# A linear-attention block and a feed-forward block in one kernel: the hand-written order of steps extended to the fifth turn

## The chip, the cores and the metric

The kernel runs on one core of a Trainium2 chip. A core has five engines with a queue each, taken strictly in order: TensorE (PE in the profile, its weight loads PEld), VectorE (DVE), ScalarE (ACT), GpSimd (POOL) and SyncE (SP), which here issues most of the transfers. The metric is the device time of one execution in microseconds (us), the median of several runs. The profile is one execution taken by the hardware profiler.

## What is computed

Per head a decaying state is updated token by token and read by a query; the result, with the heads side by side, is the input of a feed-forward block with an unusual activation.

```python
# q, k, v, f_logit: (4, 8, 768, 48), float32
f = 1.0 / (1.0 + np.exp(-f_logit))
for t in range(S):
    state = f[:, :, t, :, None] * state + np.einsum('bhd,bhe->bhde', k[:, :, t], v[:, :, t])
    y[:, :, t] = np.einsum('bhd,bhde->bhe', q[:, :, t], state)
# x: y as (3072, 384); w_in (384, 2048) and w_out (2048, 384), float64
h = x @ w_in
sp = np.maximum(h, 0.0) + np.log1p(np.exp(-np.abs(h)))
g = h * erf(sp)
out = (g @ w_out).astype(np.float32)
```

All products are made in float32.

## The kernel before

**Tiles.** The 4 x 768 tokens are 24 *chunks* of 128 tokens, numbered g; a batch has six of them. Two chunks make a *block* of 256 tokens, of which there are 12; a block's 2048 hidden columns are four *groups* of 512, and a group is made in two halves.

**Attention of a chunk.** The logits are clamped (`clamp`, DVE), turned into logarithms of the decay (ACT), and summed along the chunk by a product with a triangle (`log_sums`, PE). `decays` (ACT) makes factors from the sums, which `times_q` and `times_k` (DVE) put on the rows of q and k. Both are transposed (PE) and copied out of PSUM (`copy_q` on ACT, `copy_k`). `state_products` and `scores` (PE) make what goes into the state and the products of keys and queries; the scores are masked into `qA` (`masks`: either a masked product on DVE, or copies on ACT with a select on POOL). `add_state` (DVE) carries the state across half chunks, with the decay totals in `Tall`; `copy_state` (POOL) puts it beside v in `sv`. `x_rows` (PE, tile y) makes the rows, `copy_x` (ACT) puts them into `xT`. The totals come either from a small product (`sum_totals`) or from eight small transfers (`send_totals`, SP).

There are whole and *tiled* forms of the sums and transposes. The whole ones use the array of 128 x 128 at once, with many zeros in it (`log_sums`: one matmul of 384 columns; `transposes`: four of 128 x 128 each for q and k). The tiled ones use 64 x 64 quarters or 64-row halves (`tiled_sums`: four matmuls of 192 columns; `tiled_transposes`: sixteen of 64 columns). Tiled transposes write into a pair of PSUM banks of which there is one (`bank_pair`); `open_pair` exchanges the two single banks for it. Tiled sums need logits in another layout, which `load_f` makes with four transfers instead of one, and they use one of the two places (`ps_moe`) in which the hidden products and the output are summed.

**Feed-forward of a block.** `half_group` makes half a group of hidden columns (6 matmuls of 256 columns, tile hps); `copy_h` copies the group out (ACT); the activation takes one exp, two tanh terms and a last tanh on ACT, two combining products and a last product on DVE (`act_steps`, in turns by `act_step`). The output of blocks 0 and 1 is made directly (`project_first`, L865: 32 matmuls of 384 columns). From block 2 on `project` (L916) needs seven products of 192 columns where eight would be due; for that DVE makes sums of weights (`sum_w`) and of hidden values (`sum_h`).

**Weights** come as 16 pieces of float64 words and are rounded to float32 in seven steps each, one on ACT and six on DVE (`round_piece`).

**What sets the order.** Up to the third block an order of steps is written out by hand (`EARLY`, 454 names such as `d4` for the sums of chunk 4 or `h0_1` for a half group of block 0); it fixes each engine's queue. Behind it the loop `for it in range(2, n_blocks)` runs *turns*: turn it makes the output of block it-2 and the hidden columns of block it+1, matmul by matmul; at fixed slots of a turn it sets attention stages (`stage_d` to `stage_y`, later `burst`), loads, activation steps, sums and rounding steps. Turns 2 and 3 have rules of their own: they still round weights, use `project_first`, and pass from whole to tiled forms.

## Time and profile before

| | us |
|---|---|
| timed runs | 604.35, 605.14, 607.07; median 605.14 |
| the profiled execution: its time | 603.14 |
| the profiled execution: its span | 601.4 |
| last end of an ACT instruction of the activation | about 557 |

The span goes from the first to the last instruction of the program; what lies between it and the execution's time is start and end of the execution. In the profile, a line such as `L765` is a line of the kernel; `out<-in` are tiles. A matmul of float32 shows as two records, a transpose as one. Busy time of PE counts a matmul's full length, although matmuls overlap, so the distance from one start to the next tells its price.

### The profile page before, as it was taken

What the parts mean: (1) busy time and instruction counts of PE and PEld (TensorE: products, weight loads), DVE (VectorE), ACT (ScalarE), POOL (GpSimd) and SP (SyncE); (2) the same over time, 40 slices, a digit from 0 to 9 for tenths busy, and PEclk for the clock granted to TensorE, in tenths of its full rate; (3) what the DMA queues carried; (4) which work ended last, traced back from release to release, by engine and by line L of the source; (5) the groups of instructions that cost most, each with busy time, mean ns of one, the idle gap of its engine ahead of it and who ended that gap; (6) DMA issues with size and microseconds to landing.
All of it is one profiled execution on the core that took longest, in us unless ns stands there. A gap on an engine that the chain in (4) does not pass through costs nothing.

```text
span 601.4 us, 14264 instructions
## 1 busy us (share of the span) xinstructions
PE 581.5 (97%) x5939; PEld 507.6 (84%) x5939; DVE 429.6 (71%) x705; ACT 382.9 (64%) x483; POOL 103.5 (17%) x119
## 2 busy tenths in 40 slices
PE   8999999998799999999999999999999999999996
PEld 7787888886455778889988989989989989989996
DVE  5689889976977487596786685697695775647551
ACT  6748859787746876875866766766566646366000
POOL 1230342220404011033031010022142020000000
PEclk9899999999999999999999999999999999999999
DMA  9789974206231241232332323221311000000000
GB/s 186 212 223 255 238 176 97 43 2 158 31 76 28 55 77 19 52 72 33 71 56 34 72 34 51 52 56 27 75 29 20 26 2 1 27 1 2 27 26 31
DMA packets 152678, 41.38 MB, mean 69 GB/s; under 512 B 144416, under 2 KB 147488, under 8 KB 152608
## 3 DMA queue, kind: packets, MB, share of 16 engines
q1 hardware_dynamic: 150384, 39.81, 30.4%
q8 instruction: 49, 0.80, 0.6%
q10 hardware_dynamic: 2224, 0.59, 0.4%
q14 instruction: 21, 0.17, 0.1%
HBM read 35.59 MB, written 4.72 MB: 67 GB/s over the span
## 4 chain that ended last, share of the span: by engine, by line
PE 73%; ACT 12%; DVE 6%; DMA 3%; issue 2%; SPq 2%; POOL 1%; ACTq 0%; DVEq 0%
PE hps L765 33%; PE ops L916 22%; PE ops L865 5%; PE y L650 3%; ACT x L163 3%; PE sc L576 2%; PE sc L565 2%; PE ps_t L494 1%; DMA vt<-in_v_dram 1%; PE ps_t L484 1%; DVE Hg L722 1%; SPq L451 1%; ACT e L160 1%; DVE e L168 1%; ACT Hg L777 1%
## 5 line engine op out<-in xcount | busy, mean ns | idle before, releaser
L765 PE MATMUL hps<-xT,w_in_sb 128*128 128x256 f32 x1152 | 257.5, 381 | 4.5 <-ACT Hg L777 2.8
L765 PEld LDWEIGHTS hps<-xT,w_in_sb 128*128 128x128 f32 x1152 | 216.3, 190 | 37.5 <-ACT Hg L777 3.6
L547 POOL COPY sv<-state 48x192 f32<-48x192 f32 x88 | 87.2, 991 | 337.1 <-DVE state L542 285.2
L168 DVE SCALAR_TENSOR_TENSOR e<-x,e 128x1024 f32<-128x1024 f32 x96 | 117.3, 1221 | 15.0 <-ACT x L163 14.6
L163 ACT ACTIVATE x<-Hg,serf_bias 128x1024 f32<-128x1024 f32 x88 | 97.2, 1138 | 0.2
L160 ACT ACTIVATE e<-Hg 128x1024 f32<-128x1024 f32 x44 | 46.5, 1057 | 67.1 <-DVE Hg L722 67.0
L916 PE MATMUL ops<-wT,Hg 128*128 128x192 f32 x320 | 77.7, 326 | 0.0
L777 ACT COPY Hg<-hps 128x1024 f32<-128x1024 f32 x44 | 44.4, 1009 | 44.6 <-PE hps L765 44.2
L722 DVE TENSOR_TENSOR Hg<-Hg,e 128x1024 f32<-128x1024 f32 x44 | 53.7, 1220 | 24.3 <-ACT e L719 24.3
L916 PE MATMUL ops<-wT,scratch 128*128 128x192 f32 x288 | 67.8, 326 | 0.9 <-DVE scratch L924 0.9
L916 PE MATMUL ops<-w_out_sb,Hg 128*128 128x192 f32 x320 | 65.8, 328 | 0.0
L924 DVE TENSOR_TENSOR scratch<-scratch,ops 128x384 f32<-128x384 f32 (+1 forms) x40 | 19.9, 498 | 52.8 <-ACT scratch L932 41.9
L916 PEld LDWEIGHTS ops<-wT,Hg 128*128 128x128 f32 x320 | 56.3, 190 | 0.1
L603 DVE TENSOR_TENSOR qA<-sc,tri 64x256 f32<-64x256 f32 x68 | 28.7, 422 | 36.5 <-PE sc L576 32.8
L916 PEld LDWEIGHTS ops<-w_out_sb,Hg 128*128 128x128 f32 x320 | 53.8, 190 | 0.5
L719 ACT ACTIVATE e<-e 128x1024 f32<-128x1024 f32 x48 | 50.3, 1048 | 2.8 <-DVE e L168 2.8
L916 PEld LDWEIGHTS ops<-wT,scratch 128*128 128x128 f32 x288 | 50.3, 190 | 1.1 <-issue 1.1
L916 PE MATMUL ops<-w_out_sb,scratch 128*128 128x192 f32 x132 | 32.2, 326 | 0.0
L504 ACT COPY qA<-ps_t 64x512 f32<-64x512 f32 x48 | 27.8, 579 | 4.3 <-PE ps_t L494 2.8
L932 ACT COPY scratch<-ops 128x192 f32<-128x192 f32 x10 | 3.2, 319 | 39.5 <-PE ops L916 39.4
L650 PEld LDWEIGHTS y<-qA,sv 128*32 128x32 f32 x1408 | 21.0, 110 | 8.3 <-issue 6.2
L650 PE MATMUL y<-qA,sv 128*32 128x64 f32 x1408 | 25.0, 221 | 1.0 <-POOL sv L547 0.9
(129 smaller groups left out, 666.8 us busy)
## 6 DMA issues: line engine op xcount, KB each, us to landing
qn<-in_q_dram SPq DMA_DIRECT2D x24, 192.0 KB, 3.9
kn<-in_k_dram SPq DMA_DIRECT2D x23, 192.0 KB, 3.8
vt<-in_v_dram SPq DMA_DIRECT2D x23, 192.0 KB, 3.4
out_dram<-scratch SPq DMA_DIRECT2D x11, 384.0 KB, 2.5
sv<-in_v_dram SPq DMA_DIRECT2D x84, 48.0 KB, 2.5
w_out_sb<-in_moe_w_in_dram SPq DMA_DIRECT2D x4, 768.0 KB, 7.5
Hg<-in_moe_w_in_dram SPq DMA_DIRECT2D x4, 768.0 KB, 6.1
scratch<-in_moe_w_out_dram SPq DMA_DIRECT2D x4, 768.0 KB, 7.2
```

Of the source, the lines that this page charges most:

```text
L160: nc.scalar.activation(out=dst[:], in_=h, func=AF.Exp)
L163: nc.scalar.activation(out=dst[:], in_=h, func=AF.Tanh, bias=serf_bias[:, i : i + 1], scale=SERF_KAB[i][0])
L168: nc.vector.scalar_tensor_tensor(out=e[:], in0=x[:], scalar=SERF_KAB[i][2], in1=e[:], op0=ALU.add, op1=ALU.mult)
L547: nc.gpsimd.tensor_copy(out=svs[g1 % NSV][rows(r), r, c1, :, PAD : PAD + D], in_=state[rows(r)])
L603: nc.vector.tensor_tensor(out=to, in0=sc[half(c), r], in1=tri1[half(c)].unsqueeze(1).broadcast_to((C, HP, C)), op=ALU.mult,)
L650: nc.tensor.matmul(y[M * i : M * (i + 1), kt, half(c)], lhsT=sv[:, r, c, a, o : o + M], rhs=qA[:, r, a, half(c)], start=(c == 0 and n == 0 ...
L719: nc.scalar.activation(out=e[0][:], in_=e[0][:], func=AF.Tanh, scale=SERF_C)
L722: nc.vector.tensor_tensor(out=h, in0=h, in1=e[0][:], op=ALU.mult)
L765: nc.tensor.matmul(hts[blk, gi][:, j, :], lhsT=w_in_sb[:, kt, ft * P : (ft + 1) * P], rhs=xTs[blk][:, kt, :], start=(kt == 0), stop=(kt == ...
L777: nc.scalar.copy(out=gr["h"], in_=hts.pop((blk, gi))[:])
L865: nc.tensor.matmul(ops[:, tt, 0:d_model], lhsT=gr["h"][:, j, tt * P : (tt + 1) * P], rhs=w_out_sb[:, ft, :], start=(ft == 0), stop=(ft == ...
L916: nc.tensor.matmul(place[n], lhsT=x[:, j, :], rhs=y, start=(gi == 0 and j == 0 and n in first), stop=(gi == n_g - 1 and j == 1), skip_grou ...
```

## The change

- `EARLY` is replaced by a list of 749 steps that reaches to the start of turn 4, that is of project(2). Turns 2 and 3 and all their rules (`stages`, `weights_step`, `load_more`, `project_first`) are gone. Output of blocks 0 and 1 is in the list in parts of four matmuls (`o`), rounding of all 16 pieces (`r`), weight sums (`sw`) and the hidden sums of block 2 (`sh`).
- `SPLIT` goes from 13 to 4: tiled sums from chunk 4; the pair of banks is opened behind chunk 3 (step `op0`), so transposes are tiled from chunk 4.
- A step's name may end in a, v or g, which sets the engine of the copy: `copy_sv`, `copy_state`, `copy_k` and `copy_x` now run on ACT, DVE or POOL as the list says.
- Fillers (`z`, `keep_busy`: matmuls without use) go from 36 to 31.
- In the regular turns activation steps are at slots 4 and 8 of nine instead of 2 and 6, and logits are handled at slots 14 and 20 instead of 30 and 36. In the last turn the hidden sums of the next block start at slot 28 of 56 instead of 40, and activation steps and sums are left out of the last slots of each output.

```diff
-    FIRST, TOTALS = 3, 6
-
-    MERGE = 2 * ADJACENT
-    SPLIT = MERGE + 3
+    FIRST, SPLIT = 3, 4
...
-    def copy_sv(g, r, c):
+    def copy_sv(g, r, c, engine):
...
-        nc.scalar.copy(out=svs[g % NSV][half(1 - r), r, c, :, PAD : PAD + D], in_=pairs[:, :, r, :])
+        copy_by(engine, svs[g % NSV][half(1 - r), r, c, :, PAD : PAD + D], pairs[:, :, r, :])
...
-    def copy_state(k):
+    def copy_state(k, engine=nc.gpsimd):
...
-    def project_first(blk):
+    def project_tile(blk, gi, tt):
+
+        if (gi, tt) == (0, 0):
+            ots[blk] = ps_moe.tile([P, 2, 512], FP32, name="ops", tag="moe")
+        gr = groups[blk, gi]
+        assert gr["done"]
+        for j in range(FG):
...
     EARLY = """
-        z14 f0 k0 cl0 v0 ex0 ln0 q0 v0_00 d0 f1 v0_01 v0_10 z7 e0 k1 cl1 v0_11 qd0 k2 ex1 kd0 tq0
+        f0 f1 q0 k0 v0 z14 p2 cl0 in0 ex0 ln0 d0 z11 r2_0 cl1 e0 r2_1 f2 ex1 qd0 k1 ln1 r2_2 tq0 kd0
...
-            "d": log_sums, "e": decays, "tt": send_totals, "qd": times_q, "kd": times_k,
-            "tq": lambda g: transposes(g, "q"), "tk": lambda g: transposes(g, "k"),
+            "op": lambda n: open_pair(), "d": lambda g: log_sums(g) if g < SPLIT else tiled_sums(g), "e": decays, "tt": send_totals, "qd": times_q, "kd": times_k,
+            "tq": lambda g: transposes(g, "q") if g < SPLIT else tiled_transposes(g), "tk": lambda g: transposes(g, "k"),
...
-        for it in range(2, n_blocks):
+        for it in range(ADJACENT - 1, n_blocks):
...
-                if it < 4:
-                    step = s % 7 in (1, 4)
-                elif it == n_blocks - 1:
-                    step = s % 3 == 1
+                if it == n_blocks - 1:
+                    step = s % 3 == 1 and s % n_o < 32
                 else:
-                    step = s % 9 in (2, 6)
+                    step = s % 9 in (4, 8)
...
-                    if it == n_blocks - 1 and s % n_o == 40 and s < 2 * n_o:
+                if it == n_blocks - 1 and s % n_o == 28 and s < 2 * n_o:
```

What this does to the queues is shown at three places. The first is TensorE at the start, from the scores of chunk 2 to the first hidden product. Before (ps_t are transposes, sc<-qA scores, sc<-vt state products, sc<-ident totals, y rows, busy fillers):

```order
L576 MATMUL sc<-qA,kT 64x64 x16
L408 MATMUL busy<-tri 128x128 x7
L650 MATMUL y<-qA,sv_98 32x64 x32
L565 MATMUL sc<-vt_95,kd_108 48x48 x16
L576 MATMUL sc<-qA,kT 64x64 x16
L584 MATMUL sc<-ident,dp_110 128x2 x4
L408 MATMUL busy<-tri 128x128 x2
L765 MATMUL hps<-xT,w_in_sb 128x256 x6
```

And now, from the same scores on:

```order
L550 MATMUL sc<-qA,kT 64x64 x16
L474 MATMUL ps_t<-ident,kd_108 128x128 x4
L408 MATMUL busy<-tri 128x128 x2
L435 MATMUL ps_d<-lt,tri_60 64x192 x4
L474 MATMUL ps_t<-ident,qd 128x128 x4
L723 MATMUL hps<-xT,w_in_sb 128x256 x6
L539 MATMUL sc<-vt_95,kd_108 48x48 x16
L550 MATMUL sc<-qA,kT 64x64 x16
L616 MATMUL y<-qA,sv_98 32x64 x32
```

The first hidden product has moved ahead of the rows of chunk 2 and of chunk 3's state product and scores; ahead of it now stand the tiled sums of chunk 4.

The second place is TensorE at the output of block 0 (ops, 384 columns), around the transposes of chunk 10. Before:

```order
L565 MATMUL sc<-vt_95,kd_108 48x48 x16
L576 MATMUL sc<-qA,kT 64x64 x16
L765 MATMUL hps<-xT,w_in_sb 128x256 x3
L865 MATMUL ops<-w_out_sb,wT 128x384 x6
L484 MATMUL ps_t<-ident,qd 128x128 x4
L484 MATMUL ps_t<-ident,kd_107 128x128 x4
L865 MATMUL ops<-w_out_sb,wT 128x384 x8
L650 MATMUL y<-qA,sv_99 32x64 x32
```

Now:

```order
L823 MATMUL ops<-w_out_sb,wT 128x384 x8
L616 MATMUL y<-qA,sv_99 32x64 x32
L823 MATMUL ops<-w_out_sb,wT 128x384 x4
L723 MATMUL hps<-xT,w_in_sb 128x256 x6
L484 MATMUL ps_t<-ident,qd 128x64 x8
L484 MATMUL ps_t<-ident,kd_107 128x64 x8
L823 MATMUL ops<-w_out_sb,wT 128x384 x8
L723 MATMUL hps<-xT,w_in_sb 128x256 x6
L539 MATMUL sc<-vt_96,kd_107 48x48 x16
```

The rows of chunk 9 now stand ahead of the transposes of chunk 10, the transposes are tiled, and hidden products of block 3 stand between parts of the output.

The third place is VectorE at the same moment: what stands ahead of qd of chunk 10. Before (w_out_sb and scratch are rounding, e and Hg the activation):

```order
L364 SCALAR_TENSOR_TENSOR scratch<-scratch 128x768
L369 TENSOR_TENSOR w_out_sb<-scratch,w_out_sb 128x768
L722 TENSOR_TENSOR Hg<-Hg,e 128x1024
L168 SCALAR_TENSOR_TENSOR e<-x,e 128x1024
L346 TENSOR_SCALAR w_out_sb<-w_out_sb 128x2x2x192
L350 TENSOR_SCALAR w_out_sb<-w_out_sb 128x2x2x192
L355 SCALAR_TENSOR_TENSOR w_out_sb<-scratch,w_out_sb 128x768
L457 TENSOR_TENSOR qd<-qn_101,dp_109 128x8x48
L464 TENSOR_TENSOR kd_107<-kn_104,kd_107 128x8x48
```

Now:

```order
L364 SCALAR_TENSOR_TENSOR scratch<-scratch 128x768
L171 SCALAR_TENSOR_TENSOR e<-x,e 128x1024
L369 TENSOR_TENSOR w_out_sb<-scratch,w_out_sb 128x768
L171 SCALAR_TENSOR_TENSOR e<-x,e 128x1024
L464 TENSOR_TENSOR kd_107<-kn_104,kd_107 128x8x48
L171 SCALAR_TENSOR_TENSOR e<-x,e 128x1024
L457 TENSOR_TENSOR qd<-qn_101,dp_109 128x8x48
L680 TENSOR_TENSOR Hg<-Hg,e 128x1024
```

kd now stands two places ahead of qd, with one product of the activation between them.

More of the change, by code (lines that the diff above doesn't have):

```diff
@@ L1045, in copy_group, with next_sum, pads @@
                 steps[blk, gi] = act_steps(gr)
-            else:
-                acts.append(activate(gr))
+        own = [next(sum_places) for _ in range(NS)]
+        def next_sum(key, make, n):
+            if n == 0:
+                roundings[key] = make()
+            next(roundings[key], None)
+        def pads():
+            for t in dps:
+                nc.vector.memset(t[:, :, D:DP], 1.0)
+            for t in [qd] + kds:
+                nc.vector.memset(t[:, :, D:DP], 0.0)
+            nc.vector.memset(sc_all[:, :, HP * C : HP * (C + D)], 0.0)
         def step(n):
@@ L1065, in early @@
         for token in EARLY:
[L1066 to L1073 removed]
+            name, rest = re.match("([a-z]+)(.*)", token).groups()
+            engine = [ENGINE[rest[-1]]] if rest[-1] in ENGINE else []
+            first, *more = re.findall("[0-9]+", rest)
+            if name in "vm" and more:
+                more = more[0]
+            do[name](int(first), *map(int, more), *engine)
     with tc.manual_schedule():
```

289 lines of the change are left out of this document (101 added, 188 removed).

## Prediction

> **What bounds the kernel now.** I read three views in this order: the busy shares with the chain, the busy time by stage, and the timeline of TensorE around the places where its stages differ. First the page:
>
> ```profile
> span 601.4 us, 14264 instructions
> PE 581.5 (97%) x5939; PEld 507.6 (84%) x5939; DVE 429.6 (71%) x705; ACT 382.9 (64%) x483; POOL 103.5 (17%) x119
> PE 73%; ACT 12%; DVE 6%; DMA 3%; issue 2%; SPq 2%; POOL 1%; ACTq 0%; DVEq 0%
> ```
>
> TensorE is busy for 97% of the span and holds 73% of the chain; no other engine is above 71%. So only two things can bring time: less work on TensorE, or fewer moments in which it stands. The second is a share of 3%, some 20 us, and the view by stage tells where it lies. The columns are start:end, length, then busy time and instructions of each engine, the granted clock, the DMA share and GB/s. The cuts are: the first hidden product, the end of the old hand-ordered list, the start of project(2), the last hidden product.
>
> ```profile
> 0.00:34.80 34.80, 31.80 (x592) 26.90 (x592) 22.58 (x54) 23.97 (x49) 8.69 (x23) 0.95 0.91 202
> 34.80:139.40 104.60, 103.59 (x1124) 86.84 (x1124) 92.92 (x133) 80.31 (x115) 28.12 (x36) 1.00 0.57 139
> 139.40:230.30 90.90, 82.72 (x762) 56.99 (x760) 65.64 (x101) 64.71 (x78) 16.55 (x15) 1.00 0.34 71
> 230.30:540.80 310.50, 308.60 (x3133) 282.66 (x3132) 218.34 (x360) 201.72 (x230) 50.09 (x46) 1.00 0.20 39
> 540.80:601.40 60.60, 54.83 (x336) 54.27 (x335) 30.11 (x58) 12.15 (x14) 0.00 (x0) 0.98 0.06 21
> ```
>
> TensorE is idle for 3.0 us before its first hidden product, for 1.0 of 104.6 us in the rest of the listed part, for 8.2 of 90.9 us behind it, for 1.9 of 310.5 us in the regular turns, and for 5.8 us at the end, most of which is the output's last way out. The sore stage is the third: turns two and three, which no list covers. There VectorE is busy 65.6 of 90.9 us and ScalarE 64.7, so neither is short of time; it is their order that makes TensorE wait. Its waits, in the timeline (start, length, and in brackets the idle time ahead with what ended it):
>
> ```profile
> 141.49 0.70 PE L765 MATMUL hps<-xT,w_in_sb 128*128 128x256 f32 x2 [1.66 <-ACT Hg L777]
> ...
> 155.32 0.66 PE L484 MATMUL ps_t<-ident,qd 128*128 128x128 f32 x4 [2.36 <-DVE qd L457]
> ...
> 163.16 1.04 PE L650 MATMUL y<-qA,sv 128*32 128x64 f32 x32 [0.91 <-POOL sv L547]
> ...
> 208.57 0.46 PE L494 MATMUL ps_t<-ident,qd 64*128 64x64 f32 x8 [1.09 <-ACT xT L661]
> ...
> 221.00 5.45 PE L765 MATMUL hps<-xT,w_in_sb 128*128 128x256 f32 x24 [1.16 <-ACT Hg L777]
> ...
> 229.64 0.46 PE L494 MATMUL ps_t<-ident,qd 64*128 64x64 f32 x8 [0.85 <-ACT xT L661]
> ```
>
> These six make 8.0 of the 8.2 us. Each is an evacuation or a product that came too late on an engine with spare time: a queue order to be mended, not a resource.
>
> **The change, part by part.** *Tiled sums and transposes* come from chunk 4 instead of 13 and 11 or so: by the order, whole sums go from 13 to 4 chunks and whole transposes from 11 to 4. Their prices, from start to next start:
>
> ```profile
> 67.69 0.60 PE L484 MATMUL ps_t<-ident,qd 128*128 128x128 f32 x4
> 68.13 0.60 PE L484 MATMUL ps_t<-ident,kd 128*128 128x128 f32 x4
> 68.66 0.69 PE L576 MATMUL sc<-qA,kT 48*64 48x64 f32 x32
> ...
> 71.98 0.81 PE L424 MATMUL ps_d<-lt,tri 128*128 128x384 f32 x2
> 72.72 0.52 PE L565 MATMUL sc<-vt,kd 64*48 64x48 f32 x14
> ...
> 301.92 0.51 PE L435 MATMUL ps_d<-lt,tri 64*64 64x192 f32 x8
> 302.36 0.46 PE L494 MATMUL ps_t<-ident,qd 64*128 64x64 f32 x8
> 302.66 0.42 PE L494 MATMUL ps_t<-ident,kd 64*128 64x64 f32 x8
> 303.00 1.35 PE L765 MATMUL hps<-xT,w_in_sb 128*128 128x256 f32 x5
> ```
>
> A whole sum takes 72.72 - 71.98 = 0.74 us, a tiled one 302.36 - 301.92 = 0.44; both transposes of a chunk take 68.66 - 67.69 = 0.97 whole and 303.00 - 302.36 = 0.64 tiled. That is 9 x 0.30 + 7 x 0.33 = 5.0 us. In the merged chain view the whole sum is 0.65 and the whole transposes 0.87 us, which gives 9 x 0.21 + 7 x 0.23 = 3.5 us. I take the middle, **4.3 us**, all of it on the path, since TensorE has other work ready beside it. Everything else that TensorE does is kept: the same 480 hidden and 128 wide output records stand before project(2), in another order.
>
> Here the Trainium skill, "TensorE: Matmul & The Clock Gate", section "Part 3: Packing small matmuls", can be weighed: it says that matmuls on different row groups of the array run side by side, the span being that of one and some 4 ns for each further tile. For transposes on two row halves I estimate by that page half of 0.97 us, 0.49; the row says 0.64. By the page this part would be 7 x 0.15 = 1.1 us better, by the row not; the row is taken.
>
> *The list now reaches to project(2).* Its 749 steps replace turns two and three, so the third stage is ordered step by step like the second. If it then idles at the second stage's rate, 1.0 of 104.6 us, 0.9 us are left of the 8.2: a gain of 7.3 us. Late next are the same evacuations wherever too little of TensorE's work stands between a result and its use; for the widest wait, that of chunk 10's transposes for qd, the new order puts four wide and six hidden products between the rows of chunk 9 and these transposes, and qd is made ahead of the hidden ones. Bounds: nothing (the new order waits as long elsewhere) to 8.2 and the hidden rest. The busy time counts a matmul's whole length, so a wait costs some 0.3 us more than its bracket; six of those are 1.8, so the upper bound is 10. I take **7.5 us**, near the listed stage's row.
>
> *The start.* Five fillers fewer stand ahead of the first hidden product, and the rows of chunk 2 and the state product and scores of chunk 3 are moved behind it; against that, a weight piece of 768 KB is loaded ahead of chunk 1's inputs, and the logits of chunks 4 and 5, now in four transfers each, ahead of chunk 3's.
>
> ```profile
> 29.51 1.76 PE busy L408 x14
> ```
>
> A filler is two records: 1.76 / 7 = 0.25 us, so five are 1.25 us. The transfers, issued by SP (start and length of the issue), and TensorE's use of chunk 3's q:
>
> ```profile
> 13.81 0.70 SPq L269 DMA_DIRECT2D qn<-in_q_dram  x1
> 14.55 2.55 SPq L325 DMA_DIRECT2D w_out_sb<-in_moe_w_in_dram  x2
> ...
> 27.81 0.63 PE L484 MATMUL ps_t<-ident,qd 128*128 128x128 f32 x4
> ...
> 154.25 0.59 SPq L253 DMA_DIRECT2D lt<-in_f_logit_dram  x1
> ...
> 154.89 2.65 SPq L259 DMA_DIRECT2D lt<-in_f_logit_dram  x4
> ```
>
> Splitting costs SP 2.65 - 0.59 = 2.1 us a chunk, 4.1 for the two early ones. In before q of chunk 3 is issued at 13.81 and its transposes begin at 27.81: 14 us of cover, which hold the 4.1 us and the piece (two pieces take SP 2.55 us) too. Chunk 1's inputs have less cover. Gain of 1.25 and of the 3.0 us idle at most, loss of up to 3 us if the piece holds chunk 1 up: I take 0. The other split transfers, seven chunks x 2.1 us = 15 us on SP, lie between 35 and 200 us, long ahead of their sums.
>
> *Engines exchanged.* Copies of the state and of v go partly from POOL and ScalarE to ScalarE, VectorE and POOL:
>
> ```profile
> 159.57 3.94 POOL L547 COPY sv<-state 48x192 f32<-48x192 f32 x2 [1.53 <-DVE state L542]
> ...
> L542 DVE TENSOR_TENSOR state<-state,Tall 112x192 f32<-112x192 f32 x40 | 15.7, 392 | 1.4
> ```
>
> Two such copies took 3.9 us here and are the cause of the 0.91 us wait at 163.16; on VectorE the nearest row is the product into the state, 0.39 us. That gain is in the 7.5 already. What VectorE gets in exchange, ten such copies, is 4 us over 200, and three more copies of kT, in the 25.3 us that the third stage leaves it idle: nothing. The list's extra switches of the activation table, two in all, are hidden the same way on ScalarE.
>
> *The regular turns and the end.* Activation steps move by two slots, the sums of the last turn start at slot 28 instead of 40. TensorE loses 1.9 + 0.9 us there that waits on VectorE or ScalarE could give back:
>
> ```profile
> PE ops L916 <- DVE scratch L924: 0.9, 1, 0.9
> PE hps L765 <- DVE scratch L924: 0.8, 2, 0.6
> ```
>
> Bounds are a loss of the same 2 us and a gain of 2; I take **1.0 us**. The turns get no backlog either: up to 230.3 before has made twelve last activation products,
>
> ```profile
> L722 DVE TENSOR_TENSOR Hg<-Hg,e 128x1024 f32<-128x1024 f32 x8 | 9.8, 1221 | 9.0 <-ACT e L719 9.0
> L722 DVE TENSOR_TENSOR wT<-wT,e 128x1024 f32<-128x1024 f32 x4 | 4.9, 1236 | 0.9 <-ACT e L719 0.9
> ```
>
> and the new list ends with twelve (its steps am0_0 to am2_3).
>
> **The sum.** 4.3 + 7.5 + 0 + 1.0 = 12.8 us. The profiled execution took 603.14 us for its span of 601.4, and 603.1 - 12.8 = 590.3. The three timed runs have their median at 605.14, 2.0 us above that execution, so the forecast against it is 605.1 - 12.8 = 592.3; I give 592.
>
> **The rivals.** *The waits only move.* The old list was also made step by step and still lost 3.0 us of idle time and 36 x 0.25 = 9 us of fillers at its start; a longer one can be wrong in more places, and what was a wait on xT can become one on hps. For it: all engines are strict queues and six causes are spread over four engines. Against it: the second stage's 1%. Then only the tiled part is left: 605.1 - 4.3 = 600.8.
>
> *One transpose bank from chunk 4.* The change opens the paired bank after chunk 3, so rows y, q and k of ten chunks share one place that used to be two, and tiled sums take one of the two places of the hidden products. Rows 208.57, 221.00 and 229.64 are this regime, with waits of 0.85 to 1.16 us at a chunk's seams. If each of ten chunks waits at two seams, 1.1 + 1.2 us, that is 23 us against the 8.2 that go: 605.1 - 4.3 + 23 - 8.2 = 615.6, slower. It decides from (4.3 + 8.2) / 10 = 1.25 us a chunk; below that the change still wins. Against it: in the new order other products stand between a chunk's rows and the next transposes at nearly all places. A part of it, 10 to 16 us of waits, ends within 0.5% of before.
>
> *A cold start.* One row shows the clock granted at half:
>
> ```profile
> 20.00:40.00 20.00, 18.71 (x394) 15.59 (x395) 16.74 (x37) 11.90 (x22) 7.65 (x13) 0.91 0.81 216
> ```
>
> A share of 0.91 over 20 us at half rate is 0.09 x 20 x 2 = 3.6 us of half clock, which cost 1.8 us. With five fillers fewer a second such window may come: 592.3 + 1.8 = 594.1. The Trainium skill's page named above, "Part 1: The HAM clock gate", says that a window of about 3.4 us without enough activity halves the clock; this row agrees with the length.
>
> **How the numbers follow.** The forecast has 0.65, with its own range of 586 to 598. Moved waits have 0.19, the cold start 0.04, the shared bank in its small form 0.07 and in full 0.05. Faster by over 0.5% (below 602.1, about what a measurement here can tell from no change) is 0.65 + 0.19 + 0.04 = 0.88; same 0.07; slower 0.05. The low end takes the upper bounds, 5.0 + 10 + 4.2 + 2 = 21 us: 584. The high end takes in the moved waits: 601.
>
> **What would show it.** Tiled sums near 0.44 us and transposes near 0.64 in the early part; project(2) starting near 218 us instead of 230.3; TensorE idle about 1 us in what was the third stage; the regular turns 310 us long as before. Wrong would be a first hidden product later than 35 us, waits of L494's successor on xT or of hps on the copies at each chunk, or a project(2) that starts later than 226 us.

## The result, and the profile after

| | before | after |
|---|---|---|
| timed runs of the first measurement, median (lowest to highest) | 604.75 (602.50 to 607.07) | 586.29 (585.86 to 588.57) |
| the profiled execution, its time and span | 603.14, 601.4 | 586.41, 584.7 |
| first hidden product starts | 34.83 | 29.65 |
| project(2) starts | 230.28 | 214.20 |
| last hidden product starts | 540.41 | 521.88 |
| last product of TensorE ends | 596.50 | 577.88 |

After stands to before as 0.970 (95% interval 0.966 to 0.975): 18.5 us faster. The forecast was 592, with a range of 584 to 601; the time lies within it, 5.7 us under the forecast, on the faster side.

First the page of the kernel after, with the lines that answer to those shown of before:

```profile
span 584.7 us, 14494 instructions
...
PE 572.8 (98%) x6039; PEld 503.7 (86%) x6039; DVE 432.1 (74%) x719; ACT 383.9 (66%) x482; POOL 97.5 (17%) x108
...
PE 92%; DVE 3%; ACT 2%; DMA 1%; issue 1%; SPq 0%; DVEq 0%
```

TensorE now holds 92% of the chain where it held 73%; ScalarE's share went from 12% to 2%. TensorE's busy time fell by 8.7 us although it issues more matmuls: the tiled forms are more and smaller ones. The view by stage of the kernel after, cut at the first hidden product, the first output of block 0, project(2) and the last hidden product (columns as before):

```profile
0.00:29.60 29.60, 25.95 (x454) 22.21 (x455) 20.46 (x51) 19.52 (x38) 10.78 (x27) 1.00 0.93 190
29.60:136.00 106.40, 105.53 (x1418) 89.86 (x1417) 94.45 (x147) 88.74 (x132) 20.16 (x27) 0.98 0.69 163
136.00:214.20 78.20, 78.20 (x706) 54.96 (x705) 62.28 (x99) 53.07 (x61) 11.21 (x12) 1.00 0.39 74
214.20:521.90 307.70, 307.70 (x3130) 282.04 (x3129) 221.01 (x365) 205.38 (x233) 55.34 (x44) 1.00 0.19 37
521.90:584.70 62.80, 55.45 (x338) 54.58 (x336) 33.87 (x61) 17.15 (x19) 0.00 (x0) 0.99 0.06 20
```

The third and the fourth stage are gapless: busy time equals the length. In before's third and fourth row TensorE stood for 8.2 and 1.9 us. Before's third row begins earlier in the work than after's; counted from its own first output at 148.8, before stood for 6.5 us up to project(2). In the timeline of TensorE after, the place of before's widest wait (2.36 us for qd of chunk 10):

```profile
144.99 2.75 PE L723 MATMUL hps<-xT,w_in_sb 128*128 128x256 f32 x12
147.67 0.46 PE L484 MATMUL ps_t<-ident,qd 64*128 64x64 f32 x8
147.97 0.42 PE L484 MATMUL ps_t<-ident,kd 64*128 64x64 f32 x8
```

No bracket stands on the transposes: the hidden products ahead of them end, and qd is there. The prices of the tiled forms, further ahead in the same timeline:

```profile
85.19 0.52 PE L435 MATMUL ps_d<-lt,tri 64*64 64x192 f32 x8
85.65 0.46 PE L484 MATMUL ps_t<-ident,qd 64*128 64x64 f32 x8
85.95 0.41 PE L484 MATMUL ps_t<-ident,kd 64*128 64x64 f32 x8
86.29 2.86 PE L723 MATMUL hps<-xT,w_in_sb 128*128 128x256 f32 x12
```

A sum takes 85.65 - 85.19 = 0.46 us, the transposes of a chunk 86.29 - 85.65 = 0.64: the forecast's 0.44 and 0.64. In the view of TensorE's waits of the kernel after (sum, times, longest), all that is left is at the start, but for one at the end:

```profile
PE busy L408 <- POOL tri L1066: 1.7, 1, 1.7
PE ps_t L474 <- DVE qd L457: 1.2, 1, 1.2
PE ps_d L616 <- DVE qA L577: 0.7, 2, 0.4
PE sc L558 <- issue: 0.6, 1, 0.6
PE ops L870 <- DVE scratch L878: 0.5, 1, 0.5
PE sc L558 <- ACT qA L575: 0.2, 1, 0.2
```

By the starts in the table, 16.1 of the 18.6 us by which the last product ends earlier are won ahead of project(2), 2.4 between it and the last hidden product, 0.1 at the end. The span gained less, 16.7, because what follows the last product took 6.8 us instead of 4.9.

### The profile page after: what moved, and what is told of

Same layout as the page of the kernel before. It is cut to its first block, busy times and chain, and to the rows that moved or that the text cites. A ratio compares the mean times of both kernels' runs of the same rounds, so it can differ in the third digit from the quotient of the medians.

```text
span 584.7 us, 14494 instructions
## 1 busy us (share of the span) xinstructions
PE 572.8 (98%) x6039; PEld 503.7 (86%) x6039; DVE 432.1 (74%) x719; ACT 383.9 (66%) x482; POOL 97.5 (17%) x108
## 4 chain that ended last, share of the span: by engine, by line
PE 92%; DVE 3%; ACT 2%; DMA 1%; issue 1%; SPq 0%; DVEq 0%
PE hps L723 43%; PE ops L870 28%; PE ops L823 7%; PE y L616 4%; PE ps_t L484 2%; PE sc L550 2%; PE sc L539 2%; PE ps_d L435 1%; DMA w_out_sb<-in_moe_w_in_dram 1%; PE sc L558 1%; DVE scratch L761 1%; ACT x L166 1%; DVE qA L577 0%; PE sc L870 0%; DVE Hg L680 0%
## 5 line engine op out<-in xcount | busy, mean ns | idle before, releaser
L127 POOL COPY sv<-state 48x192 f32<-48x192 f32 x68 | 76.6, 1126 | 310.9 <-DVE state L518 239.4
L878 DVE TENSOR_TENSOR scratch<-scratch,ops 128x384 f32<-128x384 f32 (+1 forms) x40 | 19.9, 498 | 35.2 <-ACT scratch L886 26.1
L870 PEld LDWEIGHTS ops<-w_out_sb,scratch 128*128 128x128 f32 x132 | 23.3, 190 | 0.0
```

What stands on the lines that cost most here:

```text
L127: (engine.copy if engine is nc.scalar else engine.tensor_copy)(out=out, in_=in_)
L870: nc.tensor.matmul(place[n], lhsT=x[:, j, :], rhs=y, start=(gi == 0 and j == 0 and n in first), stop=(gi == n_g - 1 and j == 1), skip_grou ...
```

## The experiments

In all of them *before* and *after* are the two kernels of the change; times are medians, and the ratios are to runs of before beside them on the same chip. Where a stage is given, it is from one profile, and two profiles of the same work mostly agree within 0.6 us. The median of before was 603.94 to 604.75 us on the chips used, so differences to after of under 1 us say little.

**Whole forms again.** The new order, with whole sums up to chunk 12 and whole transposes up to chunk 10.

```diff
-        if g < SPLIT:
+        if g < 13:
...
     def tiled_sums(g):
+        if g < 13:
+            nc.tensor.matmul(dTs[g], lhsT=tri[:], rhs=lts[blk][:, j, :], start=True, stop=True)
...
+        if g < 11:
+            for i, src in enumerate((qd, kds[g % 2])):
+                for a in range(HP):
+                    nc.tensor.transpose(part[:, a, :], pairs(src)[:, a, :], ident[:])
```

> The new order with whole sums for chunks 4 to 12 and whole transposes for chunks 4 to 10, as before had them; places in PSUM and all else as in the changed kernel. Theory (TensorE is the bound everywhere, so its work counts one to one): project(2) starts 3.5 to 5.0 us later than at 214.2, no new waits, total 586.3 + 3.5 to 5.0 = 589.8 to 591.3. Rival (the tiled forms hide beside other work): project(2) within 1 us of 214.2, total within 1 us of 586.3.

Measured: 589.27 us (ratio 0.974, 0.969 to 0.980), 3.0 above after and a little under the expected 589.8. In the profile project(2) starts at 218.62, 4.4 us later than after's, and the last product ends 4.4 later too. Both executions have one half-clock window ahead of project(2), but at different places (here between 11 and 16 us, in after between 36 and 41), so only the whole way to project(2) can be compared. The view by stage of this run:

```profile
31.20:139.90 108.70, 108.14 (x1328) 90.92 (x1327) 94.21 (x147) 88.80 (x132) 22.84 (x26) 1.00 0.62 151
139.90:218.60 78.70, 78.70 (x691) 55.27 (x690) 62.35 (x99) 53.09 (x61) 11.22 (x12) 1.00 0.38 74
```

TensorE waits as little as in after; it has more to do. The rival, that the tiled forms hide beside other work, is out. The 4.4 us (3.0 by the timed runs) answer to the forecast's 4.3.

**Copies on before's engines.** Every copy of the list goes back to the engine that before used.

```diff
-        d1 q1 aq0 r2_3 v0_00g tk0 k2 v0_10g ds0 e1 cl2 v0_11g to0 r2_4 v1 ak0a kd1 z1 f3 ex2 ta0 sc0
+        d1 q1 aq0 r2_3 v0_00a tk0 k2 v0_10a ds0 e1 cl2 v0_11a to0 r2_4 v1 ak0a kd1 z1 f3 ex2 ta0 sc0
...
-        st0 ln2 z2 qd1 v2 v0_01a m0_01 d2 sp0a m0_11 q2 tq1 m0_10 v1_01g e2 tk1 m0_00 f4 z1 st1 ak1a
+        st0 ln2 z2 qd1 v2 v0_01a m0_01 d2 sp0g m0_11 q2 tq1 m0_10 v1_01a e2 tk1 m0_00 f4 z1 st1 ak1a
```

> The new order with every copy on the engine that before used (state on POOL, v and xT on ScalarE, kT on ScalarE up to chunk 8 and on VectorE from 9). Theory (the order of the steps took the waits away, the engines little): total 0 to 1.5 us over 586.3, idle time of TensorE between 136 and 214 us below 1.5 us. Rival (the exchange of engines, above all of POOL's slow state copies, made the gain): 4 to 9 us over 586.3, with waits of TensorE on POOL's sv and on the kT copies.

Measured: 585.52 us (0.968, 0.963 to 0.974); project(2) at 213.99, and TensorE is busy for 78.00 of the 78.00 us from 136 to 214. So the rival is out, and the times show no gain from the exchange of engines. A small one may be hidden: the first hidden product comes at 30.31 instead of 29.65, behind waits for copies of kT, but this execution lacks the half-clock window of after, which costs 1.7 us.

**The old slots in the regular and the last turn**, with the new list.

```diff
-                if it + 4 < n_blocks and s == 14:
+                if it + 4 < n_blocks and s == 30:
...
-                if it + 4 < n_blocks and s == 20:
+                if it + 4 < n_blocks and s == 36:
...
-                    step = s % 3 == 1 and s % n_o < 32
+                    step = s % 3 == 1
...
-                    step = s % 9 in (4, 8)
+                    step = s % 9 in (2, 6)
...
-                if it == n_blocks - 1 and s % n_o == 28 and s < 2 * n_o:
+                if it == n_blocks - 1 and s % n_o == 40 and s < 2 * n_o:
...
-                    if s % n_o < 48:
-                        sum_step()
+                    sum_step()
```

> The new list with the slots of the regular turns and of the last turn as before had them (activation steps at 2 and 6, logits at 30 and 36, last sums from slot 40, nothing left out). Theory (the moved slots took away the small waits of the turns): from the start of project(2) to project(8) 2.0 to 2.6 us more than in the changed kernel, total about 588.7. Rival (these waits were handed over by turns 2 and 3, and are gone with these): that stretch within 0.5 us, total within 1 us of 586.3.

Measured: 590.75 us (0.977, 0.971 to 0.982), 4.5 above after. From project(2) to the last hidden product it took 308.6 us, 0.9 more than after and still 1.5 less than before (the expectations, for the stretch up to project(8), had 2.0 to 2.6 or under 0.5); the end from there to the last product took 60.2 instead of 56.0, which neither expectation had. The cause is one wait in TensorE's timeline of this run, with products at double length behind it:

```profile
545.03 0.49 PE L870 MATMUL ops<-wT,scratch 128*128 128x192 f32 x2
548.83 0.98 PE L870 MATMUL ops<-wT,scratch 128*128 128x192 f32 x2 [3.31 <-DVE scratch L878]
549.60 0.85 PE L870 MATMUL ops<-wT,Hg 128*128 128x192 f32 x2
...
552.51 0.49 PE L870 MATMUL ops<-w_out_sb,scratch 128*128 128x192 f32 x2
```

Matmuls follow each other at 0.64 us a pair instead of 0.32 until 552.2. What VectorE did meanwhile:

```profile
541.62 1.22 DVE L171 SCALAR_TENSOR_TENSOR e<-x,e 128x1024 f32<-128x1024 f32 x1
...
543.76 1.22 DVE L680 TENSOR_TENSOR Hg<-Hg,e 128x1024 f32<-128x1024 f32 x1
544.90 1.22 DVE L171 SCALAR_TENSOR_TENSOR e<-x,e 128x1024 f32<-128x1024 f32 x1
546.03 0.42 DVE L761 TENSOR_TENSOR scratch<-scratch,Hg 128x256 f32<-128x256 f32 x1
...
546.83 0.42 DVE L761 TENSOR_TENSOR Hg<-Hg 128x256 f32<-128x256 f32 x1
547.16 1.52 DVE L878 TENSOR_TENSOR scratch<-scratch,ops 128x384 f32<-128x384 f32 x3
```

The additions of the output (L878) that free TensorE's place are queued behind sums of hidden values and products of the activation. Such products are there because the new list hands a small backlog on: after the last hidden product ScalarE has 17.15 us and 19 instructions left in after's last row above, 12.15 and 14 in before's. The new slots in the last turn keep these from the place of the additions.

**Fillers of the order first.** From the first output step on, rounding, activation and sums stand at the front of each window of twelve steps, as far as their order allows.

```diff
-        ax1_1 f12 st18 m9_11 r12_5 sp18g o0_0_0 c3_3 r12_6 m9_00 s9_1 q12 m9_10 r13_5 ae1_2 s9_0
+        ax1_1 f12 st18 m9_11 r12_5 sp18g r12_6 r13_5 ae1_2 at1_1 o0_0_0 c3_3 m9_00 s9_1 q12 m9_10
```

> The new list, but from the first output step on (the part that replaces turns 2 and 3) rounding, activation and sum steps go ahead of the attention steps and copies within each window of twelve steps; the same steps on the same engines, nothing else. Theory (what costs is the order in which VectorE and ScalarE serve TensorE): waits of TensorE come back between 136 and 214 us, 2 to 9 us in all, on xT, qd, qA or Hg; total 588 to 596. Rival (the waits of turns 2 and 3 came from transfers or from lack of time on the engines, not from the order): total within 1 us of 586.3.

Measured: 589.32 us (0.976, 0.970 to 0.982); 3.0 above after and inside the expected 588 to 596. The profile is of the fastest of the four executions, 586.87 us: there project(2) is 0.7 us later than after's, and 1.4 us of waits are in the stage, less than the expected 2 to 9. By the profile alone the order within a dozen steps hardly matters. The times of the other three, 588.44 to 592.93, are on the theory's side, and what they lost is in no trace; so this stays open.

**The last weight pieces loaded late.** In before ScalarE stood for piece 14's transfer; here the new list's load steps were moved to right ahead of the rounding.

```diff
-        o0_0_1 at1_1 aw1_1 r13_6 ax1_2 au1_1 p15 y9_0 y9_1 kd10 x9 o0_1_0 at1_2 ah1_1 q11 qd10 r14_0
+        at1_1 aw1_1 r13_6 ax1_2 au1_1 y9_0 y9_1 kd10 x9 o0_1_0 at1_2 ah1_1 q11 qd10 p14 r14_0 f13
```

> The new kernel, with the transfers of the last two weight pieces (14 and 15) moved in the list to right ahead of their first rounding step, as they stood in before, where ScalarE stood 2.33 us for piece 14 and TensorE waited 2.36 and 0.91 us afterwards. Theory, queue order: a late piece at the head of ScalarE's queue stops VectorE's too, so ScalarE waits 2 to 4 us near 145, waits of TensorE come back between 140 and 165, together 2 to 4 us, and project(2) starts 2 to 4 us later than 214.2; the time is 588 to 590.5. Rival, cover: the new list keeps enough of TensorE's own work ahead that a delay of 3 us in two other queues is absorbed: project(2) within 0.7 us of 214.2 and the time within 1 us of 586.3.

Measured: 585.99 us (0.971, 0.966 to 0.975). It tells nothing about the delay, which didn't come about. SP's queue runs ahead of ScalarE's: piece 14's transfer was issued at 130.35 instead of 123.44, still 12 us ahead of its rounding step at 142.72, and piece 15's at 141.00, where ScalarE waited 0.82 us instead of 0.39. In before both were issued at 139.26, 4.5 us ahead of the step that waited.

**Rounding held back in before.** Pieces 14 and 15 begin only five rounding calls later.

```diff
                 if to_round and to_round[0] in raws:
+                    n = wait[to_round[0]] = wait.get(to_round[0], 0) + 1
+                    if n <= HOLD and to_round[0] in (14, 15):
+                        return
```

> The kernel before, with one rule added: rounding of pieces 14 and 15 begins only at the sixth rounding call after the piece is due, some 5 us later, so its first step on ScalarE no longer stands in the queue ahead of a transfer that is still under way; nothing else is changed. Theory, queue order: ScalarE's wait of 2.33 us at 143.8 goes, VectorE's backlog with it, and TensorE's waits at 155.3 (2.36) and 163.2 (0.91) fall to under 0.5 together; project(2) starts 2.5 to 3.5 us earlier than 230.3, the time is 1 to 3.5 us below before's. Rival: the same VectorE work comes a little later and qd of chunk 10 is as late as before: project(2) within 1 us of 230.3.

Measured: 599.75 us (0.992, 0.989 to 0.996), 4.4 below before, more than the expected 1 to 3.5. In before stands on ScalarE, and behind it on VectorE,

```profile
143.77 0.92 ACT L344 ACTIVATE w_out_sb<-scratch 128x768 f32<-128x768 f32 x1 [2.33 <-DMA scratch<-in_moe_w_out_dram]
...
144.72 0.56 DVE L346 TENSOR_SCALAR w_out_sb<-w_out_sb 128x768 f32<-128x768 f32 x1 [5.53 <-ACT w_out_sb L344]
...
154.71 0.55 DVE L457 TENSOR_TENSOR qd<-qn,dp 128x384 f32<-128x384 f32 x1
```

and in this run, without a wait for the transfer,

```profile
144.28 0.91 ACT L344 ACTIVATE w_out_sb<-scratch 128x768 f32<-128x768 f32 x1
...
145.22 0.56 DVE L346 TENSOR_SCALAR w_out_sb<-w_out_sb 128x768 f32<-128x768 f32 x1 [3.00 <-ACT w_out_sb L344]
...
150.03 0.55 DVE L457 TENSOR_TENSOR qd<-qn,dp 128x384 f32<-128x384 f32 x1
```

TensorE in this run, at the places of before's waits for qd, sv and Hg (the other three waits are as in before, 1.66, 1.09 and 0.85 us):

```profile
153.03 0.60 PE L484 MATMUL ps_t<-ident,qd 128*128 128x128 f32 x4
...
160.34 0.64 PE L650 MATMUL y<-qA,sv 128*32 128x64 f32 x28 [0.43 <-POOL sv L547]
...
217.79 5.45 PE L765 MATMUL hps<-xT,w_in_sb 128*128 128x256 f32 x24 [1.17 <-ACT Hg L777]
```

The 2.36 us for qd are gone, the 0.91 for sv became 0.43, and project(2) starts at 227.08, 3.2 earlier. So the one wait and half of the other came from the order of the rounding steps, and in before it can be followed through three queues: a rounding step that waits for its transfer holds ScalarE, the result holds VectorE (5.53 us idle), and VectorE's qd comes late. TensorE's wait names only the last of these.

Two causes are not kept apart here. The rule also moved five of VectorE's nine rounding steps from ahead of qd to behind it, 3.9 us from start to start. VectorE's first step of the piece starts no earlier than in before (145.22 against 144.72), and qd still comes 4.7 us earlier; so in this run it was the shorter queue ahead of qd that brought it forward. In after all of VectorE's rounding of these two pieces stands behind that qd (at 144.31, the first rounding step at 145.91).

**Two more orders mended in before**, on top of that.

```diff
-        nc.scalar.copy(out=xTs[blk][:, :, j * P : (j + 1) * P], in_=yts.pop(g)[:])
+        engine = nc.vector if g == 11 else nc.scalar
+        copy_by(engine, xTs[blk][:, :, j * P : (j + 1) * P], yts.pop(g)[:])
...
-                loads[6], logits_at = it + 4, {8: it + 3, 34: it + 4}
+                loads[6], logits_at = it + 4, {8: it + 3, 50: it + 4}
```

> The kernel before with the later rounding of pieces 14 and 15, and two more orders mended in its turn 3: the logarithms of block 7's logits (two table loads and two activations on ScalarE) at slot 50 instead of 34, and the copy of chunk 11's rows to xT on VectorE instead of ScalarE. Theory, queue order: beyond what the later rounding alone brings, TensorE's waits for xT at 208.6 (1.09) and 229.6 (0.85) fall to under 0.3 each, and project(2) starts 1.3 to 2.2 us earlier than with the later rounding alone; the one at 221.0 for Hg stays within 0.6 of its 1.16 us. Rival, the waits only move: project(2) within 0.7 us of the kernel with later rounding alone, with waits elsewhere in the turn.

Measured: 601.01 us (0.995, 0.993 to 0.997), 1.3 above the held rounding alone. The ten times go from 598.98 to 604.23, and the profile is of the fastest. In it both waits for xT are gone,

```profile
203.58 0.46 PE L494 MATMUL ps_t<-ident,qd 64*128 64x64 f32 x8
...
217.36 5.45 PE L766 MATMUL hps<-xT,w_in_sb 128*128 128x256 f32 x24 [2.51 <-ACT Hg L778]
...
225.08 0.46 PE L494 MATMUL ps_t<-ident,qd 64*128 64x64 f32 x8
```

but the one for Hg grew from 1.17 to 2.51, since the logarithms and their two table loads moved in ahead of that copy on ScalarE. The second load stands two places before it:

```profile
213.82 1.28 ACT L163 ACT_TABLE_LOAD   x1
```

Of 1.94 us removed 1.34 came back. project(2) starts at 225.72, 1.36 earlier than with the held rounding alone, at the lower edge of the theory. But 0.59 of that was there ahead of the edited places (the products behind the first wait for Hg start at 141.46 instead of 142.05), which leaves 0.8, just above the rival's bound. With no gain in the times the rival, that waits only move, is the nearer one; in before these mends did not get what the list gets.

**A delay put into the new list.** ScalarE's first rounding step of piece 14 is issued four times; the values are the same.

```diff
-        nc.scalar.activation(out=dst, in_=high.bitcast(FP32), func=AF.Abs)
+        for _ in range(4 if i == 14 else 1):
+            nc.scalar.activation(out=dst, in_=high.bitcast(FP32), func=AF.Abs)
```

> The new kernel with ScalarE's first rounding step of piece 14 issued four times instead of once (the same values written again), which holds ScalarE for 3 x 0.82 = 2.5 us more at the place where it stood 2.33 us for the transfer in before. It is the delay itself that is put in here, since moving the transfer did not bring it. Theory, cover: the new list has TensorE work of its own between these results and their use, so project(2) moves by less than 0.7 us from 214.2 and TensorE's waits between 136 and 214 stay under 0.6 us. Rival, slots: the list only avoids this delay and is as brittle as before, where mending it brought project(2) forward by 3.2 us: then project(2) is 2 to 3.2 us later, with waits for qd, kd or Hg near 150 to 165.

Measured: 589.16 us (0.975, 0.972 to 0.978). In the profile, of an execution of 586.58 us, ScalarE is held 3.75 instead of 0.91 us,

```profile
143.59 3.75 ACT L345 ACTIVATE w_out_sb<-scratch 128x768 f32<-128x768 f32 x4
```

and TensorE waits 0.27 us in the whole stage; project(2) starts at 214.43, 0.2 later. The profile speaks for cover. The other three runs, 589.13 to 590.86, lie at least 2.5 us above the profiled one, the median is 2.9 us above after's, as much as the delay, and what they lost is in no trace. So the step was issued eight times:

```diff
-        for _ in range(4 if i == 14 else 1):
+        for _ in range(8 if i == 14 else 1):
```

> As the kernel with ScalarE's step of piece 14 issued four times, but eight times: ScalarE is held 7 x 0.94 = 6.6 us instead of 2.8. With 2.8 us the profile had project(2) only 0.23 us later, while the timed runs had their median 2.9 us above the new kernel's. Theory, cover: a delay of up to some 3 us is taken up, what goes beyond it is passed on: project(2) 2 to 4 us later than 214.2, with waits of TensorE for qd, Hg, xT or the output's place near 150 to 170 that sum to the same 2 to 4 us; the time 588.5 to 590.5. Rival, no limit near: project(2) within 1 us of 214.2, the time within 1 us of the kernel with four. Second rival, brittle (the timed runs of the kernel with four being the rule and its profile the exception): project(2) 5 us or more later, the time 591.5 or more.

Measured: 591.68 us (0.979, 0.975 to 0.982), above the expected 588.5 to 590.5. TensorE's timeline:

```profile
158.57 0.69 PE L551 MATMUL sc<-qA,kT 48*64 48x64 f32 x32
161.40 0.46 PE L485 MATMUL ps_t<-ident,qd 64*128 64x64 f32 x8 [2.14 <-DVE qd L458]
...
162.22 9.45 PE L824 MATMUL ops<-w_out_sb,wT 128*128 128x384 f32 x24
```

Of 6.6 us of delay 2.14 reach TensorE, and a spell of the half clock follows: the 24 records take 9.4 us where after's at this place (157.88 to 165.82) take 7.9. The stage from the first output to project(2) is 82.3 us long instead of 78.2, 4.1 more; project(2) is 5.8 later, since 1.6 us were lost ahead of the stage, where the edit doesn't reach. By the bounds put down beforehand this is the second rival, brittle (5 us or more, 591.5 or more); without those 1.6 us it is the upper edge of the theory.

What takes a delay up can be read from after:

```profile
145.91 0.55 DVE L346 TENSOR_SCALAR w_out_sb<-w_out_sb 128x768 f32<-128x768 f32 x1
...
153.61 0.55 DVE L457 TENSOR_TENSOR qd<-qn,dp 128x384 f32<-128x384 f32 x1
```

ScalarE's step is done at 144.71, 1.2 us before VectorE takes it up, and qd of chunk 11 is ready at 154.16, 3.1 us before its transposes start at 157.25. That is 4.3 us of cover, against 6.6 - 2.1 = 4.5 us that were taken up in this execution; the 2.8 us of the run before fit in. By the times, though, 2.9 us of the 2.8 and 5.4 of the 6.6 arrive. So the cover stands in the traces; why the times lose more than it leaves over is open. The 3.2 us of the held rounding in before can't be set against this, since that rule moved VectorE's steps too.

**The new slots in before**, with its own list.

```diff
-            loads, logits_at = {n - 20: it + 5}, {36: it + 4}
+            loads, logits_at = {n - 20: it + 5}, {36 if it < 4 else 20: it + 4}
...
-                    step = s % 3 == 1
+                    step = s % 3 == 1 and s % n_o < 32
...
-                    step = s % 9 in (2, 6)
+                    step = s % 9 in (4, 8)
...
-                    if it == n_blocks - 1 and s % n_o == 40 and s < 2 * n_o:
+                    if it == n_blocks - 1 and s % n_o == 28 and s < 2 * n_o:
...
-                    elif s < n_o or s % 3 == 0 or it == n_blocks - 1:
+                    elif it == n_blocks - 1:
+                        if s % n_o < 48:
+                            sum_step()
+                    elif s < n_o or s % 3 == 0:
```

> The kernel before with the new slots of the regular and the last turn (activation steps at 4 and 8 of nine, logits at 14 and 20, in the last turn sums from slot 28 and nothing in the last slots); the old list and turns 2 and 3 stay. Theory: the slots are worth some 1 us by themselves wherever they stand: the stretch from project(2) to the last hidden product 309 to 309.4 instead of 310.1, the end from there on within 0.5 us of 56.1, the time 0.5 to 1.5 us below before's. Rival: they only suit the new list's backlog; in before they change nothing (within 0.4 us) or add waits, and the gain of 2.4 us in the regular turns was handed on by the list.

Measured: 605.86 us (1.002, 1.000 to 1.005). From project(2) to the last hidden product 310.0 us, as before: TensorE's two waits for the output's place there (0.59 and 0.18) are gone, one of 0.44 whose releaser the profile doesn't show has come. The end takes 57.2 instead of 56.1, by one wait:

```profile
561.48 0.92 PE L916 MATMUL ops<-w_out_sb,Hg 128*128 128x192 f32 x4 [1.99 <-DVE scratch L924]
```

By themselves the slots give nothing; they pay only with the new list.

**No fillers.** The new list without its 31 filler products.

```diff
-        f0 f1 q0 k0 v0 z14 p2 cl0 in0 ex0 ln0 d0 z11 r2_0 cl1 e0 r2_1 f2 ex1 qd0 k1 ln1 r2_2 tq0 kd0
+        f0 f1 q0 k0 v0 p2 cl0 in0 ex0 ln0 d0 r2_0 cl1 e0 r2_1 f2 ex1 qd0 k1 ln1 r2_2 tq0 kd0 d1 q1
```

> The new kernel without any of its 31 filler products (all z steps gone from the list). Theory: the fillers stand where TensorE would be idle and only keep its clock up; without them the first hidden product starts within 1 us of 29.65, and what they decide is whether the half-clock windows of 3.4 us come: each costs 1.7 us if TensorE is the bound in it, 0 to 3 windows more at the start, so the time is 585 to 591. Rival: the fillers are on the path, 31 x 0.25 = 7.7 us, and part of it is gained: the first hidden product 2 us or more earlier, the time below 584.5.

Measured: 592.51 us (0.979, 0.975 to 0.983), 6.2 above after, and in the profile, of 594.72 us, the first hidden product starts at 38.81 instead of 29.65. Neither theory had that. TensorE's timeline without fillers:

```profile
18.99 1.65 PE L424 MATMUL ps_d<-lt,tri 128*128 128x384 f32 x2
20.43 1.06 PE L474 MATMUL ps_t<-ident,qd 128*128 128x128 f32 x4
...
22.28 1.08 PE L616 MATMUL ps_d<-qA,sv 128*32 128x64 f32 x32
...
25.25 0.66 PE L616 MATMUL ps_d<-qA,sv 128*32 128x64 f32 x32
```

and with them, in after:

```profile
16.48 0.81 PE L424 MATMUL ps_d<-lt,tri 128*128 128x384 f32 x2
17.13 0.60 PE L474 MATMUL ps_t<-ident,qd 128*128 128x128 f32 x4
```

Without fillers the same sum takes 1.65 us and four transposes 1.06, until a product at 25.25 is back to 0.66. TensorE runs at half speed from its first product at 5.97 to about 25 us, and falls back to it after that: its granted clock is 0.79, 0.84 and 0.50 in the next three stretches of 5 us.

**Only the first fillers.** The runs of 14 and 11 stay, the six single ones go.

```diff
-        st0 ln2 z2 qd1 v2 v0_01a m0_01 d2 sp0a m0_11 q2 tq1 m0_10 v1_01g e2 tk1 m0_00 f4 z1 st1 ak1a
+        st0 ln2 qd1 v2 v0_01a m0_01 d2 sp0a m0_11 q2 tq1 m0_10 v1_01g e2 tk1 m0_00 f4 st1 ak1a y0_0
```

> The new kernel with the two large runs of fillers kept (14 ahead of the first sum, 11 behind it) and the six single ones gone. Theory: what the fillers buy is the full clock from the start; once TensorE runs at it, small gaps do no harm: the first hidden product within 0.8 us of 29.65 (the six are 1.5 us of work that fills idle time), products at their short lengths (0.6 us for four transposes) from 11 us on, the time 585 to 587.5. Rival: the six hold the clock too; without them it falls for a window or more in the first 30 us, some products there take double their time, and the first hidden product is 1.5 to 4 us later than 29.65.

Measured: 587.46 us (0.972, 0.969 to 0.975), the first hidden product at 29.70 and project(2) at 214.23. TensorE's busy time ahead of it falls from 25.95 to 24.69 us, its idle time rises by as much, and the half-clock window between 36 and 41 us stays the only one. The first runs of fillers buy the full clock; the single ones stand in idle time and do nothing that the profile shows.

## Why the forecast was right, and where it was short

**Tiled forms: 4.3, measured 4.4** in the profile of the run with whole forms, 3.0 in its timed runs. The prices were read from before and came out alike. The estimate by the Trainium skill, "TensorE: Matmul & The Clock Gate", section "Part 3: Packing small matmuls", of 0.49 us for a chunk's transposes doesn't hold here; they take 0.64.

**The list over turns 2 and 3: 7.5, measured 8.2 and, with a hidden rest, up to 10.** The forecast left the third stage the second's rate of idling, 0.9 us. It has none: 78.20 of 78.20 us busy. The 10 adds the forecast's estimate that a wait costs 0.3 us more than its bracket; the held rounding bears it out, where brackets fell by 2.8 us and the stretch from the first output to project(2) by 3.5. The mechanism, a queue order to be mended, is shown by the held rounding for two of the six waits (3.2 us at project(2) from one rule), and by after's timeline, which has none. Mending two more orders gave only 0.6 net of waits. That the list does more than the sum of mended places because it sets TensorE work of other kinds between a result and its use fits the traces (2.8 us between qd of chunk 10 and its transposes, some 4 us of cover for the delays put in); the times of the runs with delays don't bear it out as clearly, so it is not shown. The wait for sv, which the forecast laid to POOL's slow copies, needed no other engine: it halved with the held rounding, and the new list has no such wait with before's engines either.

**The start: 0, and 1.7 to 3.5 left over.** That is what is left of 16.1 - 4.4 - (8.2 to 10), not a measurement of the start. Ahead of its first hidden product TensorE stands for 3.65 us in after and 3.0 in before, so no idle time was won there. Up to project(2) its idle time fell from 12.2 to 4.5 us and its busy time from 218.1 to 209.7, of which fillers are 1.4 (11.7 and 10.3). Whether five fillers fewer are part of the gain isn't shown: after's six single ones cost nothing, before's were not taken out. The transfers that the forecast set against the gain did not hold the start up: the first hidden product came 5.2 us sooner, part of it because it was moved ahead of other work. Which moves give the rest was not tried.

**The regular turns and the end: 1.0, measured 2.5.** Here the reason was wrong in part, not only the size. The forecast gave the gain to the slots, and said that the turns get no backlog, because both kernels have made twelve last products by project(2). By the first and middle steps they have not: up to project(2) before has made 14 exps and 28 tanh terms, after 12 and 24. The list leaves more of the activation behind, and the old slots of the last turn then cost 4.2 us, by the run with the old slots. The new slots alone make before no faster. So list and slots belong together: the old slots lose 0.9 of the 2.4 us in the turns, and the other 1.5 came with the list. The traces name the waits. Of before's 1.9 us there 0.77 are waits for VectorE's additions, as the forecast had it, and the new slots take these away in both kernels (0.65 with the new list and the old slots). The other 1.13 is one wait at 322.9, between two records of the same transposes, for which the profile shows no releaser. It stands near this place in all four profiles with before's list (0.37 to 1.13) and in none with the new one; why is open.

**The sum.** 12.8 was forecast, 18.5 measured: short by 0.1 in the first term, by 0.7 to 2.5 in the second, by 1.7 to 3.5 in what is left over and by 1.5 in the turns. All four fell to the same side, and 586.29 stands at the edge of the forecast's own 586 to 598. The bounds held (their upper sum was 21) but for the turns, where 2.5 stands against 2.

**The rivals.** That the waits only move happens in large part, but in before's way of mending. The shared bank costs nothing that the profile of after shows: TensorE has no wait from 37 us to project(2). A second half-clock window did not come: there is one, as in before, only at another place (between 36 and 41 us, behind a wait of 0.65).

## What to carry to other kernels

Where the bounding engine idles for a tenth of a stage (here 8.2 of 90.9 us) while no other is full, follow its wait past the engine that it names: the cause may stand two queues further, here a rounding step at the head of ScalarE's queue that waited for a transfer. Then count what else stands ahead of the late result in its own queue; an edit that mends one can move the other. Judge an order by the delay that it can take up, and test this by putting one in, and don't go by the profiled execution alone: in three of the runs here it was the fastest. Slots tuned for one state of the queues are no gain by themselves: try each half of a change without the other.

## What the runs showed of the hardware

- TensorE starts at half speed and can stay there: without fillers for 19 us, though the records have it busy for 14.72 of the 19.30 us from 5.90 to 25.20, and for 5.00 of the 5.00 us from 20 to 25. The column of the granted clock reads 1.00 in this stretch; only the lengths of the products show it. The Trainium skill, "TensorE: Matmul & The Clock Gate", section "Part 1: The HAM clock gate", says that the half clock is the default and that a busy window of about 3.4 us releases it; the double lengths agree, and by that reading the window that ended near 25 us was the first that was busy enough. How busy a window has to be, no run here shows.
- A half-clock spell can follow a wait of TensorE, and need not: behind the 3.31 us with the old slots it lasted from 548.8 to 552.2, 3.4 us, in which the products lose half, 1.7 us. Behind the 2.14 us with eight rounding steps there was one too, behind the 2.51 us with two more orders mended there was none.
- From the last product's end to the span's end it takes 4.9 to 5.0 us in some executions and 6.6 to 6.8 in others of nearly the same kernel. In after's last 6.0 us and before's last 4.1 no engine is busy, and the transfers' share is 0.12 and 0.16: the last store is landing. This is noise of 1.9 us in the span, to be left out when two spans are compared.
